# The last four projection tiles formed among the attention steps, and value units from step 18

## The chip, the cores and the metric

The kernel runs on one core of a Trainium2 chip. The metric is the device time of one execution in microseconds, the median of several runs.

## The reference

Two attentions over the same 2048 x 576 input are mixed by a gate. Each has 32 heads of 18 columns; in the second all heads share one key and one value head.

```python
x = A_x
g = _sigmoid((x * gate_w).sum(-1, keepdims=True))
# A: q, k, v of 32 heads from x @ wqkv
p = _softmax(einsum("bhqd,bhkd->bhqk", q, k) * Dh ** -0.5)
a = einsum("bhqk,bhkd->bhqd", p, v) ... @ wo_A
# B: q of 32 heads from x @ wq; one k = x @ wk and one v = x @ wv
b = (the same with the shared k and v) ... @ wo_B
return g * a + (1 - g) * b
```

## The kernel before

Products are made from high and low parts: each operand is split into a rounded part (h) and the rest (l), and three of the four products are added. A projection is 14 matmuls (`PROJ`): 128 rows of weights (a tile, `mt`) against 512 columns of x, summed in one PSUM bank. The weights of the keys, queries and the gate make 14 tiles (`MT`); tile 0 holds the shared key, the gate, the shared value and the first queries, the last tiles the queries and keys of the last heads.

*First stage.* x is loaded, split and kept in SBUF. Tiles 0 to 2 are projected as x arrives, then tiles 3 to 9 (28 projections, the loop over `tiles_left`). `project` runs the matmuls; `leave` (L162 and on) copies the result on ACT, takes the rest on DVE and stores both to `qk_d` in DRAM by POOL's queue. For tiles with keys, `kd_d` gets the difference of key columns 512 to 1023 and 0 to 511. Beside each projection `bring_row` issues one load on SP (now and then two) of the 27 that bring the first heads' rows back from `qk_d`. `load_wv` and `store_wv` split the value weights and store them to `wv_d` here.

*Lead.* Sixteen more projections (tiles 10 to 13), each followed by six maxima of head 0 and 1: a score matmul (L478) and a DVE reduction (L487). `leave_lead` copies on ACT and splits on POOL. `store_x` puts the split x into `x_d`.

*Steps.* 64 heads of 16 steps; head u takes steps 16u to 16u+15. A step makes the scores of 128 keys by 2048 queries: four matmuls (L530), four exponentials on ACT (L538), 16 value matmuls in quarters into `acc` (L544). Beside it run the maxima of the head that comes 22 steps later (`LEAD`), with one ACT copy (L481) and one fused DVE reduction (L484) in two steps. At the end of a head's maxima `max_rows` reduces them, splits them on POOL (`mh`, L118 and L120), and sends them through DRAM (`m_d`) into the rows of `qs` that the scores read.

The order of all instructions is written out by hand in three strings. `PLAIN` covers two steps, `SPARSE` eight steps with one unit (`U`), `DENSE` two steps with one unit. A unit is a piece of other work in a generator: `value_units` (32 units, each 14 matmuls of 288 columns, an ACT copy at L444 and a store) from step 10 (`VB`) to 265, and the output projection (12 matmuls a unit) from step 522. All steps from 266 to 521 are plain. `begin(T)` runs, every two steps, what `when(T, ...)` has put down for them: loads of the rows of a later head (`load_q`, `load_k`, `next_kd`), of values (`load_vg`), the openings of pools, and one piece of the `slow` work (normalising the sums of finished heads on POOL, splitting output weights).

Almost all loads and stores of the steps are issued by SP, in program order. Tiles from a pool with few buffers make the next writer wait for the last reader.

Of the kernel before, what the change touches and what calls it, by code (L numbers as in the profile page):

```python
# [8 lines left out]
F32 = mybir.dt.float32  # L9
F32R = mybir.dt.float32r  # L10
# [32 lines left out]
def gated_mix_kernel(ctx: ExitStack, tc: tile.TileContext, xT, wall, wv, wo, out):  # L43
# [3 lines left out]
    def dma(o, i, eng=None):  # L47
        o, i = (x.bitcast(F32) if x.dtype == F32R else x for x in (o, i))
        return (eng or nc.sync).dma_start(o, i)
# [16 lines left out]
    r_d = dram.tile([NU, S], F32, name="r_d")  # L66
    v_d = dram.tile([16, P, H * 19], F32, name="v_d")
    x_d = dram.tile([P, 2 * NKT - 1, S], F32, name="x_d")
    wv_d = dram.tile([2, 2, P, NKT * 288], F32, name="wv_d")
    on_d = [dram.tile([9 * P, S], F32, name=f"on{x}") for x in "hl"]  # L70


# [49 lines left out]
    def load5(t, src, rest=None):  # L122
        dma(t[:, 0:4, :], src[0:512, :].rearrange("(p k) m -> p k m", p=P))
        dma(t[0:64, 4, :], src[512:576, :], rest)
        dma(t[64:128, 4, :], src[512:576, :], rest)

    def split_w(st, w, eng_l):
        nc.scalar.activation(w["h"], st, AF.Copy)
        eng_l.tensor_tensor(w["l"], st, w["h"].bitcast(F32), op=OP.subtract)
# [89 lines left out]
    def bring_row():  # L219
        if rows_back:  # L220
            rows_back.pop(0)()

    with tc.tile_pool(name="xs", bufs=1, side="right") as xsp:
# [67 lines left out]
        for c in range(4):  # L291
            for mt in range(3):
# [10 lines left out]
                if mt == 0:  # L303
                    keep = done
                    if c == 3:
                        WN = prep_w(W.pop(0))
    vws = ExitStack()
    vwp = vws.enter_context(tc.tile_pool(name="vwp", bufs=1, side="right"))


    def load_wv(hf):
        t = vwp.tile([P, NKT, 288], F32, name="vwst")
        load5(t, wv[:, 288 * hf:288 * hf + 288])
        return t

    def store_wv(hf, st):
        w = {y: vwp.tile([P, NKT, 288], F32R, name=f"vw{y}") for y in "hl"}
        split_w(st, w, nc.vector)
        for i, y in enumerate("hl"):
            dma(wv_d[hf, i], w[y].rearrange("p k f -> p (k f)"), nc.gpsimd)  # L320

    def store_x(i):
        y, c = "hl"[i % 2], i // 2
# [7 lines left out]
    for u in range(3):  # L331
        load_q(u, put=later)

    LEAD_T = MT - 4

    def tiles_left(WN):
        for mt in range(3, MT):
            w = WN
            if mt + 1 < MT:
                WN = prep_w(W.pop(0))  # L340
            if mt + 3 < MT:
                W.append(load_w(mt + 3))
            for c in range(4):
                yield mt, c, w

    left = tiles_left(WN)
    for n in range(4 * (LEAD_T - 3)):
        mt, c, w = next(left)
        if n in (0, 10):
            vs = load_wv(n // 10)  # L350
        project(mt, c, w)
        bring_row()
        if c == 3:
            bring_row()
        if n in (8, 18):
            store_wv(n // 10, vs)
    assert not rows_back
    vws.close()


    small = ctx.enter_context(tc.tile_pool(name="small", bufs=1, side="left"))
# [35 lines left out]
    def open_ph2():  # L397
        ph1.close()
        L["pt"].append(ctx.enter_context(tc.tile_pool(name="ppool", bufs=10, side="left")))
        L["work"] = ctx.enter_context(tc.tile_pool(name="work", bufs=2, side="left"))  # L400
        p2 = ctx.enter_context(tc.tile_pool(name="p2", bufs=1, side="right"))
        L["pool"] = p2
        L["ks"] = [p2.tile([P, S], F32R, name=f"ksa{i}") for i in range(2)] + [ksb]
        L["kds"] = [p2.tile([P, 512], F32R, name="kda"), kdb]

        L["early"] = ExitStack()
        L["vx"] = L["early"].enter_context(tc.tile_pool(name="vx", bufs=1, side="right"))
        for t in L["ks"][:2]:
            for b in (SB, MB):
                dma(t[b + 54:b + 56, :], ones_r)  # L410

    def open_oacc():
        L["early"].close()
        L["oacc"] = ctx.enter_context(tc.tile_pool(name="oacc", bufs=1, side="right")) \
            .tile([P, 16, D], F32, name="oacc")

    def value_units():

        pool = L["vx"]
        XV = {}  # L420

        def load(st_):
            XV[st_] = pool.tile([P, 2 * NKT - 1, P], F32R, name="xv", bufs=2)
            dma(XV[st_], x_d[:, :, st_ * P:(st_ + 1) * P])

        load(0)
        w = [{y: pool.tile([P, NKT, 288], F32R, name=f"vw{y}{hf}") for y in "hl"} for hf in range(2)]
        for hf in range(2):
            for i, y in enumerate("hl"):
                dma(w[hf][y], wv_d[hf, i].rearrange("p (k f) -> p k f", k=NKT))  # L430
        vst = [pool.tile([P, 16, 19], F32, name=f"vst{i}") for i in range(2)]
        for t in vst:
            nc.gpsimd.memset(t, 1.0)
        yield
        for st_ in range(16):
            if st_ < 15:
                load(st_ + 1)
            x = XV.pop(st_)
            for hf in range(2):
                fp = ps_m.tile([P, 512], F32, name="pm")  # L440
                for n, (a, b, k, kr) in enumerate(PROJ):
                    nc.tensor.matmul(fp[:, 0:288], x[:kr, k if b == "h" else NKT + k, :], w[hf][a][:kr, k, :],  # L442
                                     start=(n == 0), stop=(n == len(PROJ) - 1))
                nc.scalar.activation(vst[hf][:, :, 0:18], fp[:, 0:288].rearrange("p (h d) -> p h d", d=18), AF.Copy)  # L444
                dma(v_d[st_, :, 304 * hf:304 * hf + 304], vst[hf].rearrange("p h d -> p (h d)"))
                yield
# [214 lines left out]
    def out_proj(t0, rows, first=False):  # L661

        nt = len(rows)
        oacc = L["oacc"]
        fin = t0 == 8
        O = {}

        def load(q):
            for x, y in enumerate("hl"):
                if fin:  # L670
                    O[q, y] = L["end"][y][:, 256 * q:256 * q + 256].rearrange("p (t s) -> p t s", t=1)
                    continue
                t = L["pool"].tile([P, nt, 256], F32R, name=f"oi{y}", bufs=2)
                dma(t, on_d[x][P * t0:P * (t0 + nt), 256 * q:256 * q + 256]
                    .rearrange("(t p) s -> p t s", p=P))
                O[q, y] = t

        load(0)
        yield
        w = WO[t0]  # L680
        for q in range(8):
            if q < 7:
                load(q + 1)
            o = {y: O[q, y] for y in "hl"}
            for s2 in range(2):
                st_ = 2 * q + s2
                for hf in range(2):
                    ops = [(o[b][:r, t, s2 * P:(s2 + 1) * P], w[a][:r, t, 288 * hf:288 * hf + 288])
                           for a, b in PRODS for t, r in enumerate(rows)]
                    fp = unit_bank()  # L690
                    for n, (x, y) in enumerate(ops):
                        nc.tensor.matmul(fp[:, 0:288], x, y, start=(n == 0), stop=(n == len(ops) - 1))  # L692
                    dst = oacc[:, st_, 288 * hf:288 * hf + 288]
                    if first:
                        nc.scalar.activation(dst, fp[:, 0:288], AF.Copy)
                    elif fin and hf == 0 and st_ in ON_ACT:
                        tmp = L["work"].tile([P, 288], F32, name="tmp", tag="ol", bufs=1)
                        nc.scalar.activation(tmp, fp[:, 0:288], AF.Copy)
                        nc.gpsimd.tensor_tensor(dst, tmp, dst, op=OP.add)
                    else:  # L700
                        nc.vector.tensor_tensor(dst, fp[:, 0:288], dst, op=OP.add)  # L701
                    if fin and st_ == 15:
                        dma(out[st_ * P:(st_ + 1) * P, 288 * hf:288 * hf + 288], dst, nc.sync if hf else nc.scalar)
                    elif fin and hf:
                        dma(out[st_ * P:(st_ + 1) * P, :], oacc[:, st_, :], nc.scalar if st_ in (8, 10, 12) else nc.sync)
                    yield
# [56 lines left out]
    def when(T, f):  # L763
        at.setdefault(T, []).append(f)
# [15 lines left out]
    for t in range(8):  # L780
        when(16 * (last_head(t) + 1) + 5, lambda t=t: slow.append(normalise(t)))
    when(16 * (NU - 1) + 4, lambda: run(normalise(8, at_end=True)))
    VB = 10
    when(VB - 8, lambda: (todo.append(value_units()), pull(1)))
    when(VB + 8 * 32 + 8, open_oacc)
    SEG = ((0, [P] * 4, 450, 518), (4, [P] * 4, 862, 942))
    for t0, rows, Ta, Tb in SEG:
        when(Ta, lambda t0=t0, rows=rows: slow.append(prep_wo(t0, rows)))
        when(Tb, lambda t0=t0, rows=rows: (todo.append(out_proj(t0, rows, first=t0 == 0)), pull(1)))
# [128 lines left out]
    while pos["s"] < 4 * (NSTEP - LEAD):  # L918
        T = pos["s"] // 4
        if (T + LEAD) % 16 == 0 and (T + LEAD) // 16 - 1 < NU:  # L920
            max_rows((T + LEAD) // 16 - 1)
        if T >= SEG[1][3] + 4:
            emit(DENSE, 1)
        elif any(b <= T < b + 8 * 32 for b in (VB, SEG[0][3] + 4)):
            emit(SPARSE, 1)
        else:
            emit(PLAIN if T > 2 else PLAIN.replace("sm sy sm", "smf syf smf"))
# [44 lines left out]
```

## Time and profile before

| | |
|---|---|
| median of 3 runs | 2738.71 us (2738.68 to 2739.05) |
| profiled execution, its own time | 2739.16 us |
| its span, first to last instruction | 2737.4 us |
| PE, PEld, DVE, ACT, POOL busy | 2729.2, 1301.5, 2391.7, 2443.6, 271.4 us |
| granted TensorE clock | 1.0 throughout |
| DMA | 242.09 MB, mean 88 GB/s |

PE is TensorE's matmuls, PEld its weight loads, which overlap the matmuls. A busy PE is modelled from pipelined matmuls and isn't PE at its peak. In groups, "out<-in ... xN | busy, mean ns | idle before" gives the time a group kept its engine busy, the mean of one instruction, and the time its engine stood idle before it with what ended that.

### The profile page before, as it was taken

The numbers are of one execution on the slowest core, as the hardware profiler recorded it, in microseconds if no ns is written. First come the engines' busy times: TensorE is split into PE (matmuls) and PEld (weight loads), VectorE is DVE, ScalarE is ACT, GpSimd is POOL, SyncE is SP. The second block draws the span as 40 slices with busy tenths as digits, with TensorE's granted clock in tenths as the row PEclk, the third lists the DMA queues.
The fourth block names the chain that finished last, engine by engine and source line by source line (L and its number), as shares of the span: only waits on it lengthen the run. The fifth ranks groups of instructions, "written<-read, shape, count | busy, mean of one in ns | idle before, by whom it ended". The sixth has DMA issues, their size and how long they took to land.

```text
span 2737.4 us, 60422 instructions
## 1 busy us (share of the span) xinstructions
PE 2729.2 (100%) x23542; PEld 1301.5 (48%) x23542; DVE 2391.7 (87%) x4495; ACT 2443.6 (89%) x4787; POOL 271.4 (10%) x407
## 2 busy tenths in 40 slices
PE   9999999999999999999999999999999999999999
PEld 8874444454454333333334444444444333334555
DVE  4488888888889999999999898888989999998883
ACT  4338999999999999999999999999999999998776
POOL 2371000010001000100110001000100011011002
PEclk9999999999999999999999999999999999999999
DMA  8883211122111101211133213222321223224312
GB/s 285 326 303 125 60 55 38 59 80 75 42 57 57 56 27 34 65 48 31 47 95 108 87 58 95 93 70 75 100 87 46 68 86 99 67 79 120 101 46 89
DMA packets 145954, 242.09 MB, mean 88 GB/s; under 512 B 53650, under 2 KB 99810, under 8 KB 134092
## 3 DMA queue, kind: packets, MB, share of 16 engines
q1 hardware_dynamic: 131268, 187.13, 22.7%
q0 software_dynamic: 13504, 49.88, 4.8%
q8 instruction: 185, 3.03, 0.5%
q10 hardware_dynamic: 896, 1.23, 0.1%
q14 instruction: 101, 0.83, 0.1%
HBM read 149.61 MB, written 79.78 MB: 84 GB/s over the span
## 4 chain that ended last, share of the span: by engine, by line
PE 99%; DMA 0%; DVE 0%; ACT 0%; issue 0%; ACTq 0%
PE acc L544 38%; PE ps L530 32%; PE pm L478 14%; PE ps L156 6%; PE pm L692 4%; PE pm L442 2%; PE acc L555 1%; PE pm L530 0%; DMA xsh<-xT 0%; PE ps L478 0%; PE ps L692 0%; DVE mx L487 0%; DMA wst<-wall 0%; ACT pt L538 0%; DVE oacc L701 0%; PE pm L739 0%
## 5 line engine op out<-in xcount | busy, mean ns | idle before, releaser
L538 ACT ACTIVATE pt<-ps 128x512 f32<-128x512 f32 x4048 | 2133.8, 612 | 119.9 <-PE pm L478 55.3
L487 DVE TENSOR_REDUCE mx<-pm 128x1 f32<-128x512 f32 x3068 | 1942.5, 684 | 193.9 <-PE pm L478 145.7
L530 PE MATMUL ps<-qs,ksb 56*128 56x512 f32 x2688 | 899.2, 436 | 0.1
L478 PE MATMUL pm<-ksb,qs 54*128 54x512 f32 x2336 | 794.7, 437 | 0.1
L530 PEld LDWEIGHTS ps<-qs,ksb 56*128 56x128 f32 x2688 | 435.0, 184 | 493.8 <-ACT pt L538 465.0
L544 PE MATMUL acc<-pt,vb 128*19 128x256 f32 (+3 forms) x6656 | 579.3, 434 | 0.1
L544 PE MATMUL acc<-pt,vg 128*19 128x256 f32 (+3 forms) x6224 | 553.8, 443 | 0.0
L530 PE MATMUL ps<-qs,ksa 56*128 56x512 f32 x1360 | 454.6, 436 | 0.1
L478 PEld LDWEIGHTS pm<-ksb,qs 54*128 54x128 f32 x2336 | 370.9, 184 | 125.5 <-DVE mx L487 57.6
L478 PE MATMUL pm<-ksa,qs 54*128 54x512 f32 x1232 | 425.9, 439 | 0.0
L484 DVE CUSTOM_DVE_ANT_0 junk<-pm,xb 128x512 bf16<-128x512 f32 x500 | 340.3, 681 | 0.2
L530 PEld LDWEIGHTS ps<-qs,ksa 56*128 56x128 f32 x1360 | 219.4, 184 | 239.4 <-ACT pt L538 221.9
L481 ACT ACTIVATE xb<-pm 128x512 f32<-128x512 f32 x500 | 307.5, 615 | 0.0
L544 PEld LDWEIGHTS acc<-pt,vb 128*19 128x19 f32 x6656 | 125.6, 97 | 216.1 <-issue 192.7
L478 PEld LDWEIGHTS pm<-ksa,qs 54*128 54x128 f32 x1232 | 198.0, 184 | 56.5 <-DVE mx L487 26.0
L544 PEld LDWEIGHTS acc<-pt,vg 128*19 128x19 f32 x6224 | 118.8, 97 | 207.1 <-issue 183.2
L118 POOL CAST mh<-mt 128x32 fp32r<-128x32 f32 x64 | 13.4, 210 | 1719.7 <-DVE mt L495 1719.7
L478 PE MATMUL pm<-kdb,qs 54*128 54x512 f32 x372 | 153.3, 412 | 0.0
L162 ACT ACTIVATE phl<-ps 128x512 fp32r<-128x512 f32 x40 | 23.9, 598 | 71.4 <-PE ps L156 56.8
L156 PE MATMUL ps<-xh,wh 128*128 128x512 f32 (+1 forms) x300 | 85.6, 384 | 0.0
L156 PE MATMUL ps<-xh,wl 128*128 128x512 f32 (+1 forms) x300 | 83.3, 376 | 0.0
L168 DVE TENSOR_TENSOR phl<-ps,phl 128x512 fp32r<-128x512 f32 x40 | 27.7, 692 | 62.7 <-ACT phl L162 46.8
(144 smaller groups left out, 1471.9 us busy)
## 6 DMA issues: line engine op xcount, KB each, us to landing
qs<-qk SPq DMA_DIRECT2D x384, 144.0 KB
qk<-phl POOLq DMA_DIRECT2D x56, 512.0 KB, 5.6
ksa<-qk SPq DMA_DIRECT2D x132, 144.0 KB
ksb<-qk SPq DMA_DIRECT2D x66, 144.0 KB
xv<-x_d SPq DMA_DIRECT2D x16, 576.0 KB
onh<-oh SPq DMA_DIRECT2D x32, 256.0 KB
onl<-ol SPq DMA_DIRECT2D x32, 256.0 KB
oih<-onh SPq DMA_DIRECT2D x16, 512.0 KB
```

The lines of the kernel that those rows point to most:

```text
L156: nc.tensor.matmul(fp[:, p0:p0 + g], w[a][:kr, k, :], X[b][:kr, k, x0 + p0:x0 + p0 + g], start=(n == 0), stop=(n == len(PROJ) - 1))
L168: nc.vector.tensor_tensor(hl[:, 1, :], fp, hl[:, 0, :].bitcast(F32), op=OP.subtract)
L442: nc.tensor.matmul(fp[:, 0:288], x[:kr, k if b == "h" else NKT + k, :], w[hf][a][:kr, k, :], start=(n == 0), stop=(n == len(PROJ) - 1))
L478: nc.tensor.matmul(pm, qs[u % 3][b:b + 54, i * P:(i + 1) * P], k, start=True, stop=True)
L481: nc.scalar.activation(MX["x", u, i], pm, AF.Relu)
L484: nc.vector.tensor_tensor_reduce(junk, pm, MX.pop(("x", u, i)), 1.0, -3e38, op0=OP.add, op1=OP.max, accum_out=MX[u][:, i, c:c + 1])
L487: nc.vector.tensor_reduce(MX[u][:, i, c:c + 1], pm, axis=AX.X, op=OP.max)
L530: nc.tensor.matmul(ps, kst(u)[b:b + 56, i * P:(i + 1) * P], qs[u % 3][b:b + 56, c * 512:(c + 1) * 512], start=True, stop=True)
L538: nc.scalar.activation(pt, ps, AF.Exp, scale=SCALE)
L544: nc.tensor.matmul(acc[32 * j:32 * j + 19, a:b], v_of(u, i), PT[u, i, j][:, a:b], start=(i == 0), stop=(i == 15), skip_group_check=True)
L555: nc.tensor.matmul(acc[32 * j:32 * j + 19, 256 * half + a:256 * half + b], v_of(NU - 1, i), pt[:, x + a:x + b], start=(i == 0), stop=(i == ...
L692: nc.tensor.matmul(fp[:, 0:288], x, y, start=(n == 0), stop=(n == len(ops) - 1))
```

## The change

The first stage now ends with tile 9: `NT = 10`, 12 projections (tiles 3 to 5) before the lead, and tiles 6 to 9 in the lead. Tiles 10 to 13 are formed among the steps by `row_units`, 28 `SPARSE` units from step 282 to 505: each tile in seven pieces of 292 columns (the last 296), from pieces of `x_d` that are loaded one unit ahead into two buffers. One ACT copy takes the PSUM bank into a row buffer of four pieces; POOL splits it; SP stores it. After the fourth piece POOL forms the key difference in that buffer, and splits and stores it in two halves through the same single buffer `rhl`. After the seventh, POOL splits the next tile's weights.

`wv_d` goes: `value_units` loads the raw value weights in four pieces through the two `vg` buffers and splits them on POOL. It is still opened at step 2, but its units begin at step 18. `bring_row` runs three times a projection. The pool of the output sums opens at step 506, and the pool of the early units is opened twice, for values and for rows.

```diff
-    for n in range(4 * (LEAD_T - 3)):
-        mt, c, w = next(left)
-        if n in (0, 10):
-            vs = load_wv(n // 10)
-        project(mt, c, w)
-        bring_row()
-        if c == 3:
+    for n in range(4 * (NT - 4 - 3)):
+        project(*next(left))
+        for _ in range(3):
             bring_row()
-        if n in (8, 18):
-            store_wv(n // 10, vs)
...
+    def row_units():
...
+        def load_xr(c):
+            XR.append(pool.tile([P, 2 * NKT - 1, 296], F32R, name="xr", bufs=2))
+            n = 296 if c == 6 else 292
+            dma(XR[-1][:, :, 0:n], x_d[:, :, cut(c)])
+
+        def next_w(mt):
+            W = {y: pool.tile([P, NKT, P], F32R, name=f"wr{y}") for y in "hl"}
+            split(WR.pop(0), W["h"], W["l"], nc.gpsimd, nc.gpsimd)
+            if mt + 1 < MT:
+                load_wr(mt + 1)
+            return W
+
+        def both(st, n):
+            hl = pool.tile([P, 2, 296], F32R, name="rhl", bufs=1)
+            split(st, hl[:, 0, 0:n], hl[:, 1, 0:n], nc.gpsimd, nc.gpsimd)
+            return hl[:, :, 0:n]
+
+        load_wr(NT)
+        load_xr(0)
+        w = next_w(NT)
+        yield
+        for mt in range(NT, MT):
+            rs = slice(mt * P, (mt + 1) * P)
+            first = pool.tile([P, 4, 292], F32, name="rst", bufs=1).rearrange("p c f -> p (c f)")
+            for c in range(7):
+                x = XR.pop(0)
+                if (mt, c) != (MT - 1, 6):
+                    load_xr((c + 1) % 7)
+                n = 296 if c == 6 else 292
+                fp = ps_m.tile([P, 512], F32, name="pm")
+                for i, (a, b, k, kr) in enumerate(PROJ):
+                    nc.tensor.matmul(fp[:, 0:n], w[a][:kr, k, :], x[:kr, k if b == "h" else NKT + k, 0:n],
+                                     start=(i == 0), stop=(i == len(PROJ) - 1))
+                b = (0, 292, 584, 876, 512, 0, 808)[c]
+                st = first[:, b:b + n]
+                nc.scalar.activation(st, fp[:, 0:n], AF.Copy)
+                dma(qk_d[:, rs, cut(c)].rearrange("a p f -> p a f"), both(st, n))
+                if c == 3:
+
+                    nc.gpsimd.tensor_tensor(first[:, 0:512], first[:, 512:1024], first[:, 0:512], op=OP.subtract)
+                    for i in range(2):
+                        d = both(first[:, 256 * i:256 * i + 256], 256)
+                        cs = slice(256 * i, 256 * i + 256)
+                        dma(kd_d[rs, 0:2, cs], d)
+                        dma(kd_d[rs, 2, cs], d[:, 0, :])
+                if c == 6 and mt + 1 < MT:
+                    w = next_w(mt + 1)
+                yield
...
         for hf in range(2):
-            for i, y in enumerate("hl"):
-                dma(w[hf][y], wv_d[hf, i].rearrange("p (k f) -> p k f", k=NKT))
+            src = wv[:, 288 * hf:288 * hf + 288]
+            main = src[0:512, :].rearrange("(p k) m -> p k m", p=P)
+            for k0, k1 in ((0, 3), (3, 5)):
+                t = L["pool"].tile([P, 16, 76], F32, name="vg", bufs=2)
+                t = t.rearrange("p a b -> p (a b)")[:, 0:288 * (k1 - k0)].rearrange("p (k f) -> p k f", f=288)
+                dma(t[:, 0:min(k1, 4) - k0, :], main[:, k0:min(k1, 4), :])
+                if k1 == NKT:
+                    for b in (0, 64):
+                        dma(t[b:b + 64, k1 - k0 - 1, :], src[512:576, :])
+                split(t, w[hf]["h"][:, k0:k1], w[hf]["l"][:, k0:k1], nc.gpsimd, nc.gpsimd)
...
-    VB = 10
-    when(VB - 8, lambda: (todo.append(value_units()), pull(1)))
-    when(VB + 8 * 32 + 8, open_oacc)
-    SEG = ((0, [P] * 4, 450, 518), (4, [P] * 4, 862, 942))
+    VB = 18
+    when(2, lambda: (todo.append(value_units()), pull(1)))
+    RB = VB + 8 * 33
+    when(RB - 8, lambda: (early("px"), todo.append(row_units()), pull(1)))
+    RE = RB + 8 * 7 * (MT - NT)
+    when(RE, open_oacc)
+    SEG = ((0, [P] * 4, 450, RE + 12), (4, [P] * 4, 862, 942))
...
-        elif any(b <= T < b + 8 * 32 for b in (VB, SEG[0][3] + 4)):
+        elif VB <= T < VB + 8 * 32 or RB <= T < RE or SEG[0][3] + 4 <= T < SEG[0][3] + 4 + 8 * 32:
             emit(SPARSE, 1)
```

More of the change, by code (lines that the diff above doesn't have):

```diff
@@ L68, in gated_mix_kernel @@
     x_d = dram.tile([P, 2 * NKT - 1, S], F32, name="x_d")
-    wv_d = dram.tile([2, 2, P, NKT * 288], F32, name="wv_d")
     on_d = [dram.tile([9 * P, S], F32, name=f"on{x}") for x in "hl"]
@@ L306, in gated_mix_kernel @@
                         WN = prep_w(W.pop(0))
[L307 to L318, printed above, removed]
-        for i, y in enumerate("hl"):
-            dma(wv_d[hf, i], w[y].rearrange("p k f -> p (k f)"), nc.gpsimd)
     def store_x(i):
@@ L332, in gated_mix_kernel @@
         load_q(u, put=later)
-    LEAD_T = MT - 4
+    NT = 10
     def tiles_left(WN):
-        for mt in range(3, MT):
+        for mt in range(3, NT):
             w = WN
-            if mt + 1 < MT:
+            if mt + 1 < NT:
                 WN = prep_w(W.pop(0))
-            if mt + 3 < MT:
+            if mt + 3 < NT:
                 W.append(load_w(mt + 3))
@@ L346, in gated_mix_kernel @@
     left = tiles_left(WN)
-    for n in range(4 * (LEAD_T - 3)):
-        mt, c, w = next(left)
-        if n in (0, 10):
-            vs = load_wv(n // 10)
-        project(mt, c, w)
-        bring_row()
-        if c == 3:
+    for n in range(4 * (NT - 4 - 3)):
+        project(*next(left))
+        for _ in range(3):
             bring_row()
-        if n in (8, 18):
-            store_wv(n // 10, vs)
     assert not rows_back
-    vws.close()
     small = ctx.enter_context(tc.tile_pool(name="small", bufs=1, side="left"))
@@ L404, in open_ph2 @@
         L["kds"] = [p2.tile([P, 512], F32R, name="kda"), kdb]
-        L["early"] = ExitStack()
-        L["vx"] = L["early"].enter_context(tc.tile_pool(name="vx", bufs=1, side="right"))
+        early("vx")
         for t in L["ks"][:2]:
@@ L410, in open_ph2, with early @@
                 dma(t[b + 54:b + 56, :], ones_r)
+    def early(name):
+        if "early" in L:
+            L["early"].close()
+        L["early"] = ExitStack()
+        L["px"] = L["early"].enter_context(tc.tile_pool(name=name, bufs=1, side="right"))
     def open_oacc():
@@ L415, in open_oacc, with cut, load_wr @@
             .tile([P, 16, D], F32, name="oacc")
+    def row_units():
+        pool = L["px"]
+        XR, WR = [], []
+        def cut(c):
+            return slice(292 * c, 292 * c + 292 if c < 6 else S)
+        def load_wr(mt):
+            WR.append(pool.tile([P, NKT, P], F32, name="wrst"))
+            load5(WR[-1], wall[mt])
+        def load_xr(c):
[42 more added lines that the diff above has]
+                yield
@@ L417, in value_units @@
     def value_units():
-        pool = L["vx"]
+        pool = L["px"]
         XV = {}
@@ L428, in value_units @@
         for hf in range(2):
-            for i, y in enumerate("hl"):
-                dma(w[hf][y], wv_d[hf, i].rearrange("p (k f) -> p k f", k=NKT))
+            src = wv[:, 288 * hf:288 * hf + 288]
[8 more added lines that the diff above has]
+                split(t, w[hf]["h"][:, k0:k1], w[hf]["l"][:, k0:k1], nc.gpsimd, nc.gpsimd)
         vst = [pool.tile([P, 16, 19], F32, name=f"vst{i}") for i in range(2)]
@@ L663, in out_proj @@
         nt = len(rows)
-        oacc = L["oacc"]
         fin = t0 == 8
@@ L679, in out_proj @@
         yield
-        w = WO[t0]
+        w, oacc = WO[t0], L["oacc"]
         for q in range(8):
```

## The prediction

> **What bounds the kernel now.** I read the page's first parts, then the busy time by stretches, then the groups by line inside each stretch, then the order of time on ACT, PE, POOL and SP. First the page:
>
> ```profile
> PE 2729.2 (100%) x23542; PEld 1301.5 (48%) x23542; DVE 2391.7 (87%) x4495; ACT 2443.6 (89%) x4787; POOL 271.4 (10%) x407
> ```
>
> PE is busy everywhere, but these spans overlap, so the number doesn't tell whether PE is short. The stretches do. The columns are PE, PEld, DVE, ACT, POOL busy time (instructions), clock, DMA share, GB/s; the first row lies in the projections of the first stage, the second in the lead, the third in plain steps, the fourth in steps with value units, the fifth in steps with output units of 12 matmuls:
>
> ```profile
> 88.38:139.15 50.77, 50.77 (x226) 42.07 (x225) 20.93 (x29) 17.84 (x29) 17.13 (x26) 1.00 0.97 371
> 142.27:207.19 64.92, 64.92 (x302) 46.01 (x304) 56.42 (x93) 20.88 (x37) 52.50 (x61) 1.00 0.79 296
> 913.08:1432.17 519.09, 519.03 (x4482) 197.47 (x4480) 500.38 (x947) 509.35 (x1009) 39.46 (x61) 1.00 0.17 51
> 313.09:835.83 522.74, 522.74 (x4943) 258.05 (x4942) 462.26 (x876) 489.02 (x963) 19.00 (x39) 1.00 0.19 58
> 1510.11:1589.45 79.34, 79.34 (x754) 38.64 (x752) 70.93 (x134) 75.18 (x149) 0.93 (x5) 1.00 0.25 75
> ```
>
> In plain steps ACT is busy 509.35 of 519.09 us, 98%: the exponentials set the pace and PE has room. With units ACT falls to 489.02 of 522.74, 94%, and DVE to 88%: there PE sets it. The groups of the third and fourth stretch count the steps, at 64 exponentials for 16 steps:
>
> ```profile
> L538 ACT ACTIVATE pt<-ps 128x512 f32<-128x512 f32 x897 | 470.0, 613 | 9.7 <-PE pm L478 2.6
> L487 DVE TENSOR_REDUCE mx<-pm 128x1 f32<-128x512 f32 x673 | 428.4, 684 | 16.4 <-PE pm L478 14.4 <-PE ps L530 0.2
> ...
> L538 ACT ACTIVATE pt<-ps 128x512 f32<-128x512 f32 x832 | 438.3, 611 | 21.8 <-PE pm L478 11.4 <-PE ps L530 0.8
> L487 DVE TENSOR_REDUCE mx<-pm 128x1 f32<-128x512 f32 x624 | 392.4, 684 | 58.7 <-PE pm L478 50.6 <-PE ps L530 7.9
> ```
>
> The ends of the stretches are the POOL casts of two heads' maxima, one a head, so they hold whole heads: 896/64 = 14 plain heads (one exponential more is cut in at an edge) in 519.09 us, 37.08 each; 832/64 = 13 heads with units in 522.74 us, 40.21 each. Eight steps take 18.54 us plain and 20.11 with a value unit, so a unit costs (40.21 - 37.08)/2 = 1.565 us. DVE's waits for PE (58.7 us against 16.4) show the same change of the bound.
>
> In the first stage ACT waits for PE at every projection, here the first and last copy of 16 projections and what ended the idle time before each:
>
> ```profile
> 88.38 0.60 ACT L162 ACTIVATE phl<-ps 128x512 fp32r<-128x512 f32 x1 [2.58 <-PE ps L156]
> ...
> 139.15 0.60 ACT L162 ACTIVATE phl<-ps 128x512 fp32r<-128x512 f32 x1 [2.58 <-PE ps L156]
> ```
>
> (139.15 - 88.38)/16 = 3.173 us a projection: PE's pace, 227 ns for each of 14 matmuls.
>
> **The change part by part.** *Sixteen projections leave the first stage*: four tiles by four column pieces. They stand on PE's path, and the lead (16 more projections with maxima) stays what it is, with tiles 6 to 9 in place of 10 to 13: -16 x 3.173 = -50.77 us. ACT's and DVE's copies and the splitting of the value weights, which leave too, lie beside that PE time (ACT 17.84 of 50.77 us busy) and give nothing more. The rule of the Trainium skill, "TensorE: Matmul & The Clock Gate", Back-to-back issue gap, puts a sustained matmul of 512 columns at about 131 ns. By it the projection is 1.83 us, the saving 29.3 us, and the sum would be 15.2 us slower; the trace disagrees, with 227 ns.
>
> *Twenty-eight row units come in*, each turning eight plain steps (282 to 505) into eight of the value unit's kind: same order of work, same 14 matmuls, one ACT copy. Base price 28 x 1.565 = 43.8 us. A row unit has 292 columns instead of 288. A bound from below is nothing; from above, four columns at the projection's 227/512 = 0.443 ns x 14 x 28 = 0.7 us. I take 0.7, since units are PE-bound: 44.5 us. As a cross-check, output units with 12 matmuls give 79.34/2 = 39.67 a head, so two matmuls cost (40.21 - 39.67)/2 = 0.27 us; the price follows the matmul count. The copy is ACT's as before:
>
> ```profile
> L444 ACT ACTIVATE vst<-pm x32: 410/412/414, 233.3 to 856.3; 128x288 f32<-128x288 f32 x32
> ```
>
> 0.41 us each lies in ACT's idle 6%, and is in the unit's price already.
>
> *POOL* gets each unit's split, two instructions of 292 columns, where plain steps hold little POOL work (39.46 of 519.09 us). Its rates, by a cast and two-input operations of 512 columns:
>
> ```profile
> L120 POOL TENSOR_TENSOR ol<-ot,oh 128x512 fp32r<-128x512 f32 x32 | 41.1, 1285 | 3.7 <-DMA onl<-ol 1.3
> L118 POOL CAST oh<-ot 128x512 fp32r<-128x512 f32 x32 | 19.5, 610 | 203.5 <-DMA onh<-oh 202.9
> L194 POOL TENSOR_TENSOR pd<-pst 128x512 f32<-128x512 f32 x4 | 5.2, 1300 | 0.1
> ```
>
> So 1.19 + 2.51 = 3.70 ns a column: 1.08 us a unit; at the fourth unit of a tile 1.30 + 2 x 0.95 more, at the last the next weights' 640 columns, 2.4 us. About 13 us in a tile's 141 us: hidden. DVE's reductions don't lengthen beside POOL: in the lead, where POOL works 52.50 of 64.92 us, the same form takes
>
> ```profile
> L487 DVE TENSOR_REDUCE mx<-pm 128x1 f32<-128x512 f32 x60 | 37.1, 680 | 0.6 <-PE pm L478 0.6
> ```
>
> against 684 ns in the steps. If POOL is late, ACT's next copy into the single row buffer would wait with the exponentials queued behind it; at the fourth unit POOL needs 1.08 + 1.30 us before the fifth copy may write, and that copy comes 20.1 us later.
>
> *SP* gets per unit an x piece (128 x 9 x 292 x 4 B = 1314 KB) and a store of 292 KB; the fourth unit adds four kd stores. Landings by the nearest rows, in us:
>
> ```profile
> qk<-phl POOLq DMA_DIRECT2D x56, 512.0 KB, 5.6
> kd<-pdhl POOLq DMA_DIRECT2D x10, 512.0 KB, 6.1
> x_d<-xh POOLq DMA_DIRECT2D x4, 1280.0 KB, 6.3
> ...
> DMA to landing us min/median/max: 3.1/5.6/13.6
> ```
>
> (The last line is the row stores' own.)
>
> The piece is asked for one unit (20.1 us) ahead and lands in 6.3, so 13.8 us are left for what SP holds before it. SP waits in order: behind a store waiting for POOL stand the next loads of q rows, and behind those the next piece. The fourth unit's chain is two waits for landing stores with POOL between: about 2 (matmuls) + 0.4 + 1.1 + 6.1 + 0.95 + 6.1 + 0.95 = 17.6 us at worst, before the next unit. I cost it at nothing, with 10 us of the next piece's slack as cover; uncovered, each us is a us of PE. Bandwidth is there: share 0.17 now, and 1.6 MB more in 20 us adds 80 GB/s to 51 where the first stage moves 371.
>
> *Value weights* are now loaded raw and split on POOL at step 2, in two buffers, before the first value unit, which moves from step 10 to 18. SP, POOL and the chain of waits around it now:
>
> ```profile
> 217.68 0.60 SPq L49 DMA_DIRECT2D xv<-x_d  x1
> ...
> 233.47 1.21 SPq L49 DMA_DIRECT2D qs<-m_d  x2
> ...
> 231.46 0.21 POOL L118 CAST mh<-mt 128x32 fp32r<-128x32 f32 x1 [12.90 <-DVE mt L495]
> ...
> 231.17 2.04 PE pm L442 x14
> ```
>
> Four pieces of 864 or 576 columns are 2 x (3.20 + 2.13) = 10.7 us of POOL, two buffers' fills stand in series, and a fill lands in 3.1 to 6.3 us. In today's clock POOL is done between about 233 and 239.5, ahead of the first unit (step 18, 231.2 + 18.5 = 249.7). Queued behind it on POOL is the cast of head 1's maximum, moved from 231.5 to 233-239.5; from that cast to its rows landing takes (234.7 - 231.5) + 3.1 to 5.6 = 6.3 to 8.8 us, and the scores want them at step 16, at 231.2 + 6 x 2.32 = 245.1. So 239.5 to 248.3 against 245.1: 0 to 3.2 us, and I take 0, nearer the middle. The move of value units itself costs nothing: 256 steps either way.
>
> *Three row loads a projection* instead of one or two: 12 projections must cover 27 issues of SP. Five take
>
> ```profile
> 95.36 5.59 SPq L49 DMA_DIRECT2D qs<-qk  x5
> ```
>
> so 27 take 30.2 us of 38.1; the first maxima need only the first fifteen. Bytes of these 12 projections: 6.29 MB of row stores, 0.79 of differences, 0.98 of weights, 3.68 of rows = 11.7 MB, 31.6 us at 371 GB/s. Hidden by the projections' 38.1 us.
>
> **The sum.** The profiled execution took 2739.16 us (span 2737.4, 1.8 around it), 0.45 above the median 2738.71. -50.77 + 44.5 = -6.3 us, with 0.3 either way for the columns: 2732.9 in a profiled execution, 2732.4 by the median.
>
> **The rivals.** *The first stage gives part back.* Now it runs at 0.97 of the DMA engines and ACT once waited there for a store:
>
> ```profile
> ACT phl L162 <- DMA qk<-phl: 5.7, 2, 5.3
> ```
>
> With the lead's 296 GB/s, the 11.7 MB need 39.7 us, 1.6 more than the matmuls; with that, or the 3.2 us of the late maximum, the gain is 3 to 5 us: 2733.8 to 2735.6, within 0.2% (5.5 us, about what a measurement of this kernel can tell from no change). For it: the forecast clears this bound by only 0.8 us. Against: those 5.3 us moved no later copy, since 16 projections kept 3.173 us on average. Chance 0.20.
>
> *SP's chain makes the next x piece late (the slower side).* After the fourth unit of a tile SP is held 17.6 us and then still has six q loads and five stores of a head and, late in the stretch, six k loads, by this row at 0.68 us an issue and up to 1.1 by the one above:
>
> ```profile
> L49 SPq DMA_DIRECT2D qs<-qk x384: 674/684/1591, 58.0 to 2587.7; - x192
> ```
>
> It decides where hold plus queue goes over 20.1 + 13.8 = 33.9 us from that unit: PE then waits for the piece, ACT and DVE behind it. Slower by 0.2% needs 6.3 + 5.5 = 11.8 us, 2.95 in each of four tiles, so 36.9 us. My count is 17.6 + 11 x 0.68 to 1.1 = 25 to 30 us, with k loads up to 36.6: under the first bound in most tiles, near it in one. Against: today's value units never wait for theirs. At 3.5 us a tile: 2732.4 + 14 = 2746.4. Chance 0.15 for it and any other wait of that size.
>
> *Projections aren't paced by matmuls.* Then their removal saves less; at ACT's 17.84 us of work in that stretch for 16 projections, saving 17.84, the result is 2765.4. The rows above speak against it: ACT waits for PE each time. Chance 0.01. The Trainium skill's spacing in "TensorE: Matmul & The Clock Gate", Back-to-back issue gap, would be a milder such case, at 2753.9.
>
> ```profile
> its engine sat idle before it (us, times) until:
>   DVE mx L487: 9.8, 31
>   issue: 0.2, 1
> ```
>
> These are the value units' matmuls (L442): idle before them came from DVE's reductions, never from a transfer.
>
> **How the numbers follow.** Forecast as summed: 0.64, all of it faster by over 0.2%; its own range 2731.5 to 2733.2. Part given back: 0.20, same. Slower: 0.16. The range takes in the forecast with a unit 2 us cheaper over all at its low end (2730) and the whole of the second case, to 2744.2; 0.16 lies above it.
>
> **What would show it.** In the changed profile: last projection copy about 51 us earlier; the cast of head 1's maximum at 180 to 189 and no PE idle after it; heads of about 40.2 us between steps 282 and 506; row units' matmuls waiting for DVE, not for DMA; POOL's busy time up by about 60 us. It is wrong if heads there take over 40.6 us, if ACT's row copies wait for POOL, or if the lead takes over 65 us.

## The result, and the profile after

The changed kernel takes 2742.95 us (median of 22 runs, 2740.42 to 2747.10) against 2738.96 before: ratio 1.0016, 95% interval 1.0010 to 1.0022. That is 4.0 us slower; I forecast 2732.4, 6.6 us faster than this median of before. Its profiled execution took 2741.43 us, 2.27 more than the one before, and its runs spread over 6.7 us where those of before spread over 2.

The page of the changed kernel, part 1:

```profile
PE 2725.0 (99%) x24158; PEld 1339.4 (49%) x24158; DVE 2367.1 (86%) x4465; ACT 2440.9 (89%) x4785; POOL 321.0 (12%) x471
```

and the engines of its chain that ended last:

```profile
PE 97%; DMA 2%; DVE 1%; SPq 0%; ACT 0%; issue 0%
```

Before, PE held 99% of that chain and DMA nothing. The first stage did what was forecast. The last projection's copy on ACT, by the order of time:

```profile
88.37 0.60 ACT L161 ACTIVATE phl<-ps 128x512 fp32r<-128x512 f32 x1 [2.57 <-PE ps L155]
```

It stood at 139.15: 50.78 us earlier. The row units' copies show where the time came back (last value unit, then units 0, 9, 10, 12, 13, 25, 26 and 27 of 28):

```profile
823.62 0.41 ACT L498 ACTIVATE vst<-pm 128x288 f32<-128x288 f32 x1 [0.45 <-PE pm L496]
863.91 0.41 ACT L448 ACTIVATE rst<-pm 128x292 f32<-128x292 f32 x1 [1.37 <-PE pm L444]
...
1045.04 0.41 ACT L448 ACTIVATE rst<-pm 128x292 f32<-128x292 f32 x1 [0.48 <-PE pm L444]
1065.75 0.41 ACT L448 ACTIVATE rst<-pm 128x292 f32<-128x292 f32 x1 [0.56 <-PE pm L444]
...
1106.09 0.41 ACT L448 ACTIVATE rst<-pm 128x292 f32<-128x292 f32 x1 [0.54 <-PE pm L444]
1126.92 0.42 ACT L448 ACTIVATE rst<-pm 128x296 f32<-128x296 f32 x1 [1.25 <-PE pm L444]
...
1368.53 0.42 ACT L448 ACTIVATE rst<-pm 128x292 f32<-128x292 f32 x1 [0.59 <-PE pm L444]
1393.77 0.42 ACT L448 ACTIVATE rst<-pm 128x292 f32<-128x292 f32 x1 [5.66 <-PE pm L444]
1414.80 0.42 ACT L448 ACTIVATE rst<-pm 128x296 f32<-128x296 f32 x1 [1.45 <-PE pm L444]
```

Undisturbed units follow each other at 20.12 us, as forecast (20.13). Four intervals are longer: 20.71, 20.83, 25.24 and 21.03. All 27 take 550.89 us, 7.65 over 27 x 20.12. About 0.6 of that is the ordinary spread of units, since a run below without any of these waits takes 543.82, so some 7.1 us are waits. From the last value unit to the first row unit pass 40.29 us, where a unit and eight plain steps make 20.11 + 18.54 = 38.65: 1.6 more. At the measured spacing 28 units cost 28 x (20.12 - 18.54) = 44.2 us (44.5 forecast). In sum -50.8 + 44.2 + 1.6 + 7.7 = 2.7; the executions differ by 2.3, so 0.4 of gain elsewhere stays unexplained.

What PE waited for stands in the chain of waits, first for units 10 and 13, then for the longest interval and the one behind it:

```profile
1051.17 9.02 DMA sm<-sum_d
...
1116.72 7.88 DMA xr<-x_d
...
1374.27 3.15 DVE mx L541 x5
...
1381.09 9.04 DMA xr<-x_d
1390.26 3.41 PE pm L444 x14
...
1404.99 7.51 DMA xr<-x_d
```

At unit 10 a head's sum (`sm`) lands late, which DVE needs; at units 13, 26 and 27 it is an x piece. The one issued at 1381.1 lands 9 us later, and PE stands. SP's queue shows why it was issued then:

```profile
1348.31 0.34 SPq L49 DMA_DIRECT2D m_d<-mh  x1
1351.52 1.25 SPq L49 DMA_DIRECT2D qs<-m_d  x2
1352.82 0.59 SPq L49 DMA_DIRECT2D xr<-x_d  x1
1353.51 0.68 SPq L49 DMA_DIRECT2D qk<-rhl  x1
1362.81 4.71 SPq L49 DMA_DIRECT2D kd<-rhl  x4
1367.57 0.36 SPq L49 DMA_DIRECT2D kda<-kd  x1
1367.97 4.56 SPq L49 DMA_DIRECT2D qs<-qk  x6
1372.57 4.33 SPq L49 DMA_DIRECT2D ksa<-qk  x6
1377.00 2.95 SPq L49 DMA_DIRECT2D ot<-oe  x4
1380.00 0.55 SPq L49 DMA_DIRECT2D sum_d<-oe  x1
1380.60 0.45 SPq L49 DMA_DIRECT2D vg<-v_d  x1
1381.09 2.06 SPq L49 DMA_DIRECT2D xr<-x_d  x1
...
1385.56 8.03 SPq L49 DMA_DIRECT2D R<-r_d  x8
1402.15 0.35 SPq L49 DMA_DIRECT2D m_d<-mh  x1
```

The key difference's stores (kd) hold SP until 1367.5, 19 loads and stores follow, and the piece comes behind them. What held the stores, and a second thing, stand on POOL:

```profile
1349.31 0.81 POOL L119 TENSOR_TENSOR rhl<-rst,rhl 128x292 fp32r<-128x292 f32 x1
...
1361.57 0.40 POOL L117 CAST rhl<-rst 128x256 fp32r<-128x256 f32 x1 [10.19 <-DMA qk<-rhl]
...
1400.35 1.29 POOL L688 TENSOR_TENSOR ot<-ot,R 128x512 f32<-128x512 f32 x1 [29.38 <-DMA R<-r_d]
1401.58 0.21 POOL L117 CAST mh<-mt 128x32 fp32r<-128x32 f32 x1
```

POOL waited 10.2 us for a row store to land. The rows were split at 1350.12, but SP issued their store only at 1353.51, behind a maximum's rows and a piece; from there it took 8.1 us. And the normalisation's multiply waits for its R loads, and the cast of a head's maximum stands behind it. Its store (m_d at 1402.15) is what SP waits for before it issues the last piece (1404.99).

### The profile page after: what moved, and what is told of

The parts are those of the page before. It is cut to its first block, busy times and chain, and to the rows that moved or that the text cites. A ratio compares the mean times of both kernels' runs of the same rounds, so it can differ in the third digit from the quotient of the medians.

```text
span 2739.5 us, 61796 instructions
## 1 busy us (share of the span) xinstructions
PE 2725.0 (99%) x24158; PEld 1339.4 (49%) x24158; DVE 2367.1 (86%) x4465; ACT 2440.9 (89%) x4785; POOL 321.0 (12%) x471
## 4 chain that ended last, share of the span: by engine, by line
PE 97%; DMA 2%; DVE 1%; SPq 0%; ACT 0%; issue 0%
PE acc L598 37%; PE ps L584 26%; PE pm L532 19%; PE ps L155 5%; PE pm L745 4%; PE pm L496 2%; PE pm L444 2%; DMA xr<-x_d 1%; PE acc L609 1%; DVE mx L541 0%; SPq L49 0%; PE pm L584 0%; DMA sm<-sum_d 0%; DMA wst<-wall 0%; PE ps L532 0%; DMA qs<-qk 0%
## 5 line engine op out<-in xcount | busy, mean ns | idle before, releaser
L532 PE MATMUL pm<-ksb,qs 54*128 54x512 f32 x2336 | 780.9, 433 | 0.7 <-DVE mx L541 0.5
L598 PE MATMUL acc<-pt,vb 128*19 128x256 f32 (+1 forms) x7104 | 568.7, 417 | 0.0
L598 PEld LDWEIGHTS acc<-pt,vb 128*19 128x19 f32 x7104 | 143.9, 97 | 222.5 <-issue 187.7
L532 PEld LDWEIGHTS pm<-kdb,qs 54*128 54x128 f32 x372 | 68.3, 184 | 0.8
L155 PE MATMUL ps<-xh,wh 128*128 128x512 f32 (+1 forms) x220 | 62.2, 381 | 0.4 <-DVE mx L541 0.3
L688 POOL TENSOR_TENSOR ot<-ot,R 128x512 f32<-128x512 f32 x32 | 41.2, 1288 | 163.2 <-DMA R<-r_d 163.2
L155 PE MATMUL ps<-xh,wl 128*128 128x512 f32 (+1 forms) x220 | 59.9, 370 | 0.0
```

Source lines behind the costliest of these rows:

```text
L155: nc.tensor.matmul(fp[:, p0:p0 + g], w[a][:kr, k, :], X[b][:kr, k, x0 + p0:x0 + p0 + g], start=(n == 0), stop=(n == len(PROJ) - 1))
L532: nc.tensor.matmul(pm, qs[u % 3][b:b + 54, i * P:(i + 1) * P], k, start=True, stop=True)
L598: nc.tensor.matmul(acc[32 * j:32 * j + 19, a:b], v_of(u, i), PT[u, i, j][:, a:b], start=(i == 0), stop=(i == 15), skip_group_check=True)
L688: nc.gpsimd.tensor_tensor(ot[:rows, cs], ot[:rows, cs], R[:rows, cs], op=OP.mult)
```

## The experiments

The theories: A, x pieces are late; B, the chain through the single buffer `rhl`; C, bandwidth; then D, POOL's and DVE's order, in which normalisation instructions wait for loads that come late by the pieces, ahead of urgent work. Times of before in these comparisons are 2738.85 to 2739.14.

**Pieces two units ahead.**

```diff
         load_xr(0)
+        load_xr(1)
...
-                if (mt, c) != (MT - 1, 6):
-                    load_xr((c + 1) % 7)
... (behind the unit's matmuls)
+                if (mt, c) < (MT - 1, 5):
+                    load_xr((c + 2) % 7)
```

> Each x piece is asked for two units ahead, right behind the matmuls that free its buffer, instead of one unit ahead. Theory A (late pieces): the excess over the forecast is PE waiting for an x piece that SP issues late and that takes 7.5 to 9 us to land; asked for 18 us earlier it lands in time, the waits at units 25 to 27 and 13 (5.1 + 0.9 + 0.7 us in the profile) go, and the time falls from 2743 by 6 to 9 us to 2734 to 2737. Rival B (the chain through the single buffer rhl): the waits stay where POOL and SP are held by stores landing one after another, whatever piece is loaded when, and the time stays at 2741 to 2745. Rival C (bandwidth: the added transfers slow the others): no change either, the same bytes move.

2741.68 us, ratio 1.0011 (1.0002 to 1.0019): 1.3 us of the 6 to 9 that A promised, and inside what B and C expected. No unit waits for a piece, yet the last interval is 26.03 us. What PE waits for there:

```profile
PE ps L585 <- DMA qs<-m_d: 3.5, 1, 3.5
```

and the chain ahead of it (pieces under 1 us left out):

```profile
1392.93 7.03 DMA R<-r_d
...
1400.02 1.29 POOL ot L689
...
1401.82 1.46 DMA m_d<-mh
...
1403.97 1.98 DMA qs<-m_d
```

R comes late, the multiply is late, the cast behind it, and now the scores of the next head wait for their maximum rows. Late pieces alone don't make the loss: A falls as the only cause. This is where D comes from.

**Two buffers for the split pieces.**

```diff
-            WR.append(pool.tile([P, NKT, P], F32, name="wrst"))
+            t = L["pool"].tile([P, 16, 76], F32, name="vg", bufs=2)
+            WR.append(t.rearrange("p a b -> p (a b)")[:, 0:NKT * P].rearrange("p (k f) -> p k f", f=P))
...
-            hl = pool.tile([P, 2, 296], F32R, name="rhl", bufs=1)
+            hl = pool.tile([P, 2, 296], F32R, name="rhl", bufs=2)
```

> The split pieces get two buffers rhl instead of one (the raw weights of the next tile go into an idle vg buffer to make room). Theory A: SP is held about 10 us less at each tile's fourth unit, so the next piece is issued earlier: at the last tile by up to 9 us, which takes most of its 5 us wait; 2736 to 2739. Rival B (the chain itself is the cause): all of it goes, 2733 to 2736. Rival C (bandwidth): stays at 2741 to 2745.

2740.77 us, 1.0006 (0.9998 to 1.0015), a smaller gain than A or B expected and 0.2 us under C's range. The wait at unit 26 is gone, but the interval of 27 is now 4.4 us too long: SP issues that piece behind the late maximum:

```profile
1400.50 0.58 SPq L49 DMA_DIRECT2D xr<-x_d  x1
```

**No reloads.**

```diff
-            n = 296 if c == 6 else 292
-            dma(XR[-1][:, :, 0:n], x_d[:, :, cut(c)])
+            dma(XR[-1], x_d[:, :, 0:296])
...
+        load_xr(0)
...
-                if (mt, c) != (MT - 1, 6):
-                    load_xr((c + 1) % 7)
+                XR.append(x)
```

> Leaves the x pieces out: two buffers are filled once and used for all 28 units, so the rows are computed from wrong columns of x and 26 loads of 1.3 MB go. All theories that blame these loads (late, or taking bandwidth from others) expect all waits of this stage gone: 2732.4 as forecast plus what a second entry from plain to sparse steps costs (1.2 to 1.6 us), so 2733.5 to 2734.5. Rival B (the chain through rhl holds ACT or POOL by itself): 2737 to 2743.

2734.47 us, 0.9984 (0.9975 to 0.9993), in the range that theories blaming the loads gave. Units stand 20.0 to 20.2 us apart, though `rhl` is single: B falls as the only cause. POOL's first wait in the chain, with no piece ahead of the row store:

```profile
1353.88 0.40 POOL L117 CAST rhl<-rst 128x256 fp32r<-128x256 f32 x1 [3.36 <-DMA qk<-rhl]
```

3.4 us instead of 10.2. The store is issued earlier, at 1350.30, and takes 3.6 us from there instead of 8.1, so the pieces do slow the store that follows one. SP's kd stores come 7.7 us earlier than in the change, and the R loads 9.8 us (1375.81 instead of 1385.56), of which 0.8 is this run being ahead by then. From first issue to the multiply the R loads take about as long (14.0 and 14.8). So R is late mostly by what SP holds ahead of it, less by being slower itself. 2734.47 is what the change takes, with its order of steps, when no piece is loaded.

**A pause in the kernel before.**

```diff
-    when(VB + 8 * 32 + 8, open_oacc)
+    when(VB + 8 * 33 + 8, open_oacc)
...
-        elif any(b <= T < b + 8 * 32 for b in (VB, SEG[0][3] + 4)):
+        elif VB <= T < VB + 8 * 16 or VB + 8 * 17 <= T < VB + 8 * 33 or SEG[0][3] + 4 <= T < SEG[0][3] + 4 + 8 * 32:
```

> The kernel before, with eight plain steps put between the 16th and the 17th value unit, nothing else. Theory (each entry from plain into sparse steps costs 1.2 to 1.6 us that the steady prices of the forecast leave out): 2739.0 + 1.4, so 2740.2 to 2740.6. Rival (the later maxima after an entry are only a shift between engines, given back at the exit): 2739.0, no change within 0.3 us.

2740.11 us, +1.26 by the medians, though the ratio 1.0005 (0.9996 to 1.0014) doesn't exclude no change. The trace shows the place. ACT's copies around the pause:

```profile
534.71 0.41 ACT L444 ACTIVATE vst<-pm 128x288 f32<-128x288 f32 x1 [0.46 <-PE pm L442]
574.56 0.41 ACT L444 ACTIVATE vst<-pm 128x288 f32<-128x288 f32 x1 [1.21 <-PE pm L442]
```

39.85 us, 1.20 over 38.65. Here a second entry from plain into sparse steps costs 1.2 us that steady prices leave out; in the changed kernel the same place took 1.6.

**Both, pieces ahead and two buffers.** The two edits above together.

> Pieces two units ahead and two buffers rhl together. After the first four runs two theories are left. Theory D (POOL's order): the multiply by R, which waits 25 to 29 us for loads that land behind the 1.3 MB pieces, stands on POOL ahead of the cast of head 31's maximum; the cast comes 9 to 12 us late and with it the rows of the next head's scores; early pieces don't mend that, so one wait of 1 to 6 us at the last unit stays: 2736 to 2740. Theory A (late pieces alone): with both edits no piece is late, so 2734.5, as without reloads.

2735.78 us, 0.9988 (0.9980 to 0.9997): 7.2 us under the change, just outside D's range and over A's 2734.5. The edits do 1.3 and 2.2 us alone, since each alone leaves one of two waits that stand at the same place. Two intervals are still long, by 1.2 us at unit 10, where a sum lands late, and by 0.5 at unit 27, at late maximum rows. Early pieces thus mend most of what D had expected to stay.

**The multiply later.**

```diff
                 r0 += n
         yield
+        if not at_end:
+            yield
```

> The changed kernel with one empty turn put between the loads of R and the multiply, so that at the last tile the multiply stands on POOL behind the cast of the head's maximum, not ahead of it; every transfer is as before. Theory D: the wait at the last unit (0.9 us here, but 4 to 6 us in the two variants) goes, the one at unit 26 from the late piece (5.1 us) stays: 1 to 3 us faster than the change, 2740 to 2742. Theory A: no difference, 2742 to 2743.5.

2740.44 us, 1.0004 (0.9995 to 1.0013), 2.5 us under the change, in D's range. POOL:

```profile
1387.33 0.21 POOL L117 CAST mh<-mt 128x32 fp32r<-128x32 f32 x1 [16.94 <-DVE mt L549]
...
1399.54 1.28 POOL L690 TENSOR_TENSOR ot<-ot,R 128x512 f32<-128x512 f32 x1 [4.85 <-DMA m_d<-mh]
```

The cast comes 14.25 us earlier than in the change (1401.58), the multiply behind it. The rows of the maximum gain only 4 us by it (their loads are issued at 1399.58 instead of 1403.62): SP sends their store behind the R loads, at 1393.26, and it lands 6.3 us later. PE's waits for the pieces of units 13 and 27 are gone and the one at unit 26 stays (4.1 us), but the interval of 27 is still 20.76. The late sum of unit 10 isn't there either; it is missing too in the runs with two buffers and with pieces issued by ACT, so it isn't put down to this edit.

**Pieces issued by ACT.**

```diff
-            dma(XR[-1][:, :, 0:n], x_d[:, :, cut(c)])
+            dma(XR[-1][:, :, 0:n], x_d[:, :, cut(c)], nc.scalar)
```

> The x pieces are issued by ACT's queue instead of SP's, at the same place of the order; same bytes, same buffers. If the waits come from order in SP's queue (pieces issued late behind SP's waits, and other loads behind the pieces), pieces are issued on time, and R, sum and maximum rows land early: the 7.7 us of waits go, less 28 issues of about 0.6 us on ACT, of which ACT's idle time in units (6%, 1.2 us a unit) covers most: 2735 to 2738. If it is bandwidth (1.3 MB beside the rest, whoever issues), R lands as late: 2740 to 2743.

2753.85 us, 1.0053 (1.0040 to 1.0066): a miss for both sides. The issues themselves (0.53 us each on ACT) cost little that the trace shows: most units stay at 20.12 us, and the way into the first took 40.94 instead of 40.29. But SP itself now waited for pieces 14 times between 860 and 1440, 78.3 us in all, where in the change it did so four times, 10.8 us. The longest came twice, here in 1370 to 1392:

```profile
SPq L49 <- DMA xr<-x_d: 9.9, 1, 9.9
```

so R, the multiply and the cast came later still, and the intervals of units 13 and 27 took 23.8 and 37.4 us. Why SP waits for a piece that ACT issued isn't settled, and so this run doesn't part bandwidth from the order of queues.

**No plain steps between the units.**

```diff
+        elif VB + 8 * 32 <= T < RB:
+            emit(SPARSE, 0)
```

> The changed kernel with the eight steps between value and row units written in the sparse order without a unit, so that there is no second entry from plain into sparse steps. From the run with a gap in the kernel before (+1.26 us): 1.3 us faster than the change, 2741.4 to 2741.9. If the entry's cost comes from the unit's own work after a pause rather than from the order of steps: no difference.

2739.76 us, 1.0002 (0.9993 to 1.0011): 3.2 us less, more than expected; the waits differ too (unit 26: 23.65 us instead of 25.24), so the total of this run can't price the entry.

**All waits.** Pieces ahead, two buffers, and empty turns for t = 2 and 3:

```diff
... (ahead of the reciprocals, and again ahead of the multiply)
+        if t in (2, 3):
+            yield
```

> Pieces two units ahead, two buffers rhl, and for the two normalisations that fall among row units (t = 2 and 3) one empty turn before the reciprocals and one before the multiply by R. Theory D (POOL and DVE stand, in their own order, at instructions that wait for loads behind the pieces): the two waits left with both edits (1.2 us at a late sum, 0.6 us at late maximum rows) go: 2735.8 - 1.8 = 2734.0, the time without reloads. Rival (bandwidth slows everything a little): stays at 2735 to 2736.

2734.58 us, 0.9984 (0.9975 to 0.9993): the time without reloads, with all of them in place. The last value unit, the first and the last row unit:

```profile
824.48 0.41 ACT L500 ACTIVATE vst<-pm 128x288 f32<-128x288 f32 x1 [0.44 <-PE pm L498]
864.70 0.41 ACT L450 ACTIVATE rst<-pm 128x292 f32<-128x292 f32 x1 [1.32 <-PE pm L444]
...
1408.52 0.42 ACT L450 ACTIVATE rst<-pm 128x296 f32<-128x296 f32 x1 [0.51 <-PE pm L444]
```

543.82/27 = 20.14 us a unit, and none over 20.23: no wait is left. So C falls as well: all pieces are loaded, and the time is within 0.1 us of the run without them. The runs lie within 1.2 us of each other, where those of the change spread over 6.7. Of the 8.4 us between the change and this run the two edits to the pieces and buffers give 7.2 and the turns 1.2.

**The same without the pause.**

> The same, and the eight steps between value and row units in the sparse order without a unit. Entry theory: 1.3 us less than the same with the gap, 2732.7. The larger step of the changed kernel by this edit (3.2 us) would then be other waits that moved. If it repeats here (2730.8), the entry costs more than the run on the kernel before showed.

2733.99 us, 0.9982 (0.9973 to 0.9990), the fastest here, though only 0.6 us under the last. From the last value unit to the first row unit:

```profile
823.62 0.41 ACT L500 ACTIVATE vst<-pm 128x288 f32<-128x288 f32 x1 [0.45 <-PE pm L498]
862.99 0.42 ACT L450 ACTIVATE rst<-pm 128x292 f32<-128x292 f32 x1 [0.49 <-PE pm L444]
```

39.37 us instead of 40.22. Less a unit of 20.11, eight sparse steps without a unit take 19.3 us, more than plain ones (18.54), which eats part of what the entry costs.

## Why the prediction was wrong

*Right.* The first stage gave 50.78 us (50.77 forecast). Units took 20.12 us where nothing waited (20.13). The value weights' splits were done and the cast of head 1 came at 185.5, inside 180 to 189, with no wait of the scores after it. No part of the first stage's gain was given back, so that rival fell. The time still lies in the stated range, which reached to 2744.2 for that rival's sake: this is luck.

*Wrong: SP's chain, costed at nothing.* This is the step that failed. It put the chain at 17.6 us from the fourth unit's start and a piece's landing at 6.3, and left out of the sum that its own upper count, 36.6, was already over its limit of 33.9. At the last tile the chain took 21.3 us (1346.2 to 1367.5). Of its two waits for a landing, 6.1 each in the count, the second was only 2.6, but the first was 10.2, since the row store went out late and landed slowly. The 19 issues behind it took 13.5 us, so the piece was asked for 34.9 us after the unit's start, 1.0 over the limit, and landed in 9.0, which is 2.7 more: together about the 3.8 us that PE waited, with 1.3 more in slow matmuls (last section). The rival on the slower side had this mechanism, with its k loads, in the tile that it called near. It came in that tile alone: the pieces of units 13 and 27 (0.7 and 0.9 us) were issued behind a maximum's rows, which POOL had made late.

*Wrong: POOL, called hidden.* I summed POOL's busy time and asked who waits for its copies. I didn't ask what stands behind its waits: the multiply already waited for R in the kernel before, ahead of a cast:

```profile
1395.38 1.29 POOL L634 TENSOR_TENSOR ot<-ot,R 128x512 f32<-128x512 f32 x1 [18.29 <-DMA R<-r_d]
1396.61 0.22 POOL L118 CAST mh<-mt 128x32 fp32r<-128x32 f32 x1
```

There the two heads around it took 74.4 us by their casts (1357.81 to 1432.17), hardly more than two plain ones (74.2). In the change R came later, and the cast came 14 us later than it does with the multiply behind it. The run with the multiply later shows this order at work, and the one with all waits mended shows its size once the pieces are early: 1.2 us, together with the late sum on DVE. That sum is of the same kind, but it stands only in some executions (0.6 us in the change, 1.2 with both edits).

*Left out: the entry.* Steady prices by whole heads can't show a cost paid once; one more piece of sparse steps brings one more, 1.2 us in the kernel before and 1.6 here.

The run without reloads sets the split: 2734.47 of 2742.95, so 8.5 us of the miss are waits that the pieces cause, and the 2.1 us between 2732.4 and 2734.5 are the entry and 0.5 to 0.9 of small terms that no run tells apart.

## What to carry to other kernels

For each load that a change adds to an in-order queue, look not only at its own deadline but at every instruction that already waits for a load of that queue, and at what stands behind it on its engine. Two waits that end at the same place hide each other: an edit that removes one gains little alone, and only both together show what either is worth. An instruction moved forward on its engine gains no more than the queue behind it lets through: a cast came 14 us earlier here and its rows 4. Steady rates price a longer stretch, not the number of times that the order of work changes.

## What the runs showed of the hardware

A long wait of PE cost more than its length. The granted clock is the third column from the end; these stretches lie before, in and after the wait for the piece at unit 26:

```profile
1385.00:1388.00 3.00, 1.48 (x14) 0.60 (x6) 2.83 (x7) 2.69 (x6) 0.00 (x0) 1.00 1.05 328
1388.00:1390.20 2.20, 0.00 (x0) 0.00 (x0) 0.00 (x0) 0.12 (x1) 0.00 (x0) 0.89 0.97 338
1390.20:1393.70 3.50, 3.44 (x16) 3.31 (x16) 0.00 (x0) 0.00 (x0) 0.00 (x0) 0.58 0.34 96
```

The waits name its length as the longest of three:

```profile
PE pm L444 <- DMA xr<-x_d: 5.4, 3, 3.8
```

The clock was 0.58 in the 3.5 us after it, and the unit's 14 matmuls took 3.41 us where an undisturbed unit takes 2.1: 1.3 us of the 5.1. Behind the waits of 0.7 and 0.9 us the matmuls took 2.15 and 2.13. The Trainium skill, "TensorE: Matmul & The Clock Gate", Part 1, says that TensorE falls to half its clock after an idle window of about 3.4 us. The wait of 3.8 us here agrees. In narrower stretches of the traces the clock fell to 0.50 here 3.2 us after PE stopped, and stayed there for 3.4 us. But the delay isn't fixed, nor is 3.4 us a safe length: with pieces two units ahead the clock fell 1.5 us into a wait of 3.5 us and stayed down for 6.8, which cost 5.9 us in all, and with two buffers it fell 4.2 us after a wait of 3.2 us had begun, when PE was already back at work.
